# Turning three of the four tiles of x with VectorE instead of TensorE, in a kernel that mixes sliding-window attention with an MLP

## The chip, the cores and the metric

The kernel runs on one core of one Trainium2 chip. The metric is the device time of one execution in microseconds (us). Before the change the median of three executions is 770.48 us (769.53 to 770.53).

## What is computed

The input x has 2048 tokens of 512 features, in float32. Two branches read it and a gate per token mixes them:

```python
g = sigmoid((x * gate_w).sum(-1, keepdims=True))
# branch a: attention, 32 heads of 16 features, causal, a window of 256 tokens
qkv = x @ wqkv                       # (2048, 512) @ (512, 1536)
scores = q @ k.T * 16 ** -0.5        # masked to 0 <= query - key < 256
a = softmax(scores) @ v  @ wo
# branch b: MLP of width 1792
b = gelu(x @ w1 + b1) @ w2 + b2
out = g * a + (1 - g) * b
```

## The kernel before

**Tiles.** The tokens are cut into four tiles of 512 (`T`, numbered t = 0 to 3 in the code, the first to the fourth in the text). Every product that must keep float32 accuracy is taken as three passes: each operand is split into a rounded high part and the remainder as a low part, and `mm3` (lines 89 to 92) issues high x high, high x low and low x high. One call with 512 columns is three matmuls.

**The features must lie on the partitions.** TensorE contracts over partitions, so the projections need x with features on partitions and tokens along the row: `xts[t]`, 4 chunks of 128 features, a high and a low part, 512 tokens. In memory x lies the other way round, token by token. `load_xr` (line 186) loads a tile as four blocks of 128 tokens by 512 features into buffers of the tags `tmp` (three blocks) and `raw` (one block). `qkv_x` (line 191) then, block by block, lets TensorE turn the four 128x128 pieces with an identity (line 204) into one PSUM bank, lets ScalarE copy the bank as the high part (line 208) and VectorE subtract for the low part (line 211). The same four row blocks feed the gate: `gate` (line 216) has `gate_z` (line 228) multiply each with the gate's weights and sum along the row on VectorE, and `gate_end` (line 221) makes g and 1 - g.

**The stage of projections.** `qkv(t)` (line 284) computes for a tile twelve pieces of four `mm3` calls: eight for q and k (line 234), four for v (line 256), numbered n = 0 to 11. Each piece uses one of two PSUM banks of the tag `d`. A q or k piece is taken out by ScalarE (line 248) and VectorE (line 251) into one of eight buffers of the tag `h`, and stored to DRAM (line 252); a v piece by ScalarE (line 271), and stored (line 273). While tile t is projected, the next tile of x is loaded after n = 0 (n = 1 for the first tile), turned after the pieces n in `xat` (5, 7, 8, 9 for the first tile, 4, 6, 8, 10 for the others), and its gate follows. In the first tile the weights come in at the same time: `load_raw` (line 121) loads 256 KB, and `split` (line 140) makes the two parts, high on ScalarE, low on VectorE or GpSimd. The turned tile is also stored to DRAM (`XT`, line 304) for the MLP, which runs later.

**After that.** Attention starts when a set amount of the dense work is done (`START`, `AHEAD`); from there on `fill` interleaves what is left of the dense work, the last tile's projections and the MLP, with attention, and the rest of the output follows. VectorE finds the row maxima of attention (line 399).

**What sets the order.** TensorE, ScalarE, VectorE and GpSimd execute in the order in which the program emits their instructions. Emission is steered by a plan of times: `after(ns, fn)` puts a piece of work so many planned nanoseconds later, `tick` advances the plan. All DMAs are issued by SyncE (SP), in one queue whose order a scheduler chose beforehand; an issue that must wait holds up everything behind it. Each DMA signals one of eight counters in turn, and a DMA waits until the one eight places ahead of it has landed, so at most eight are under way.

Of the kernel before, what the change touches and what calls it, by code (L numbers as in the profile page):

```python
# [9 lines left out]
F32 = mybir.dt.float32  # L10
F32R = mybir.dt.float32r
BF16 = mybir.dt.bfloat16
AF = mybir.ActivationFunctionType
# [4 lines left out]
S, D, F, H, DH, W = 2048, 512, 1792, 32, 16, 256  # L18
T = 512
NT = S // T  # L20
NB = T // 128
NC = D // 128
# [10 lines left out]
def gated_mix(ctx: ExitStack, tc: tile.TileContext, x, wqkv, wo, w1, b1, w2, b2, gate_w, out):  # L33
    nc = tc.nc
    x = x[0]
# [3 lines left out]
    sb = ctx.enter_context(tc.tile_pool(name="sb", bufs=1))  # L39
    dr = ctx.enter_context(tc.tile_pool(name="dr", bufs=1, space=DRAM))  # L40
    ps = ctx.enter_context(tc.tile_pool(name="ps", bufs=1, space=PSUM))
# [3 lines left out]
    def f32(ap):  # L45
        return ap.bitcast(F32)
# [39 lines left out]
    g = cp.tile([128, S // 128], F32, name="g")  # L86
# [8 lines left out]
    now, todo, done = [0.0, 0], [], set()  # L95

    def after(ns, fn, *args):
        now[1] += 1
        heapq.heappush(todo, (now[0] + ns, now[1], fn, args))
# [7 lines left out]
    def tick(ns):  # L107
        now[0] += ns
        while todo and todo[0][0] <= now[0]:
            step_todo()  # L110

    def need(*keys):
        for key in keys:
            while key not in done:
                step_todo()
# [5 lines left out]
    def load_raw(key, early=False):  # L121
        kind, i = key
        src = {"qk": lambda: wk4[:, :, i * 128:(i + 1) * 128],
               "v": lambda: wqkv[i * 128:(i + 1) * 128, 2 * D:3 * D],
               "w1": lambda: w1k[:, :, i * 128:(i + 1) * 128],
               "w2": lambda: w2[i * 128:(i + 1) * 128],
               "wo": lambda: wo[i * 128:(i + 1) * 128]}[kind]()
        if early and kind == "v":
            if i == 0:
                raws["v"] = f32(sb.tile([128, NC, 2, T], F32R, tag="xt", bufs=1, name="raw_v"))  # L130
            raw = raws["v"][:, i, 0]
        elif early:
            raw = sb.tile([128, 2, 320], F32, tag="pt", bufs=PTS, name=f"raw_{kind}{i}")
            raw = raw.rearrange("p a b -> p (a b)")[:, 0:T]
        else:
            raw = sb.tile([128, T], F32, tag="raw", bufs=3, name=f"raw_{kind}{i}")
        nc.sync.dma_start(raw.rearrange("p (c f) -> p c f", c=NC) if len(src.shape) == 3 else raw, src)
        raws[key] = raw

    def split(key, eng):  # L140

        kind, i = key
        raw = raws.pop(key)
        w = sb.tile([128, 2, T], F32R, tag="w", bufs=14, name=f"{kind}_{i}")
        nc.scalar.activation(w[:, 0], raw, AF.Copy)
        wt[key] = w.rearrange("p s (c f) -> p s c f", c=NC) if kind in ("qk", "w1") else w

        def lo():
            eng.tensor_sub(w[:, 1], raw, f32(w[:, 0]))
            done.add(("w", key))  # L150
        after(700, lo)
# [3 lines left out]
    def load(key):  # L155

        paced[0] = max(now[0], paced[0] + PACE)
        after(paced[0] - now[0], load_now, key)
# [17 lines left out]
    def clear_k(i):  # L176

        pr, n = divmod(i, 4)
        for s in range(2):
            v = of_head(ks[:, pr, n * 1024:(n + 1) * 1024], s)  # L180
            nc.scalar.activation(v, nil.unsqueeze(2).unsqueeze(3).broadcast_to([128, 4, 2, 64]), AF.Identity,
                                 bias=own[:, 2 * pr + s:2 * pr + s + 1])

    xts, xrs = {}, {}

    def load_xr(t):
        for b in range(NB):
            xrs[t, b] = sb.tile([128, D], F32, tag=("tmp", "raw")[b // 3], bufs=3, name=f"xr{t}_{b}")
            nc.sync.dma_start(xrs[t, b], x[t * T + b * 128:t * T + (b + 1) * 128])

    def qkv_x(t, b):

        if b == 0:
            if t < NT - 1:
                v = (ks[:, 0], ks[:, 1], qs.rearrange("p a c -> p (a c)"))[t]
                v = v.rearrange("p (c s t) -> p c s t", c=NC, s=2)
            else:
                v = sb.tile([128, NC, 2, T], F32R, tag="xt", bufs=1, name=f"xt{t}")
            xts[t] = v
        xt = xts[t]  # L200
        xr = xrs[t, b]
        p = ps.tile([128, NC, 128], F32, tag="sm", bufs=3, name=f"xp{t}_{b}")
        for c in range(NC):
            nc.tensor.transpose(p[:, c], xr[:, c * 128:(c + 1) * 128], ident)
        tick(4 * 110)

        def hi():
            nc.scalar.activation(xt[:, :, 0, b * 128:(b + 1) * 128], p, AF.Copy)

        def lo():  # L210
            nc.vector.tensor_sub(xt[:, :, 1, b * 128:(b + 1) * 128], p,
                                 f32(xt[:, :, 0, b * 128:(b + 1) * 128]))
            done.add(("x", t, b))
        after(100, hi), after(500, lo)

    def gate(t):
        for b in range(NB):
            after(1500 * b, gate_z, t, b)
        after(6500, gate_end, t)

    def gate_end(t):
        sl = slice(t * NB, (t + 1) * NB)
# [2 lines left out]
        nc.vector.reciprocal(g[:, sl], g1[:, sl])  # L225
        nc.vector.tensor_scalar(g1[:, sl], g[:, sl], -1.0, 1.0, op0=ALU.mult, op1=ALU.add)

    def gate_z(t, b):
        xr = xrs.pop((t, b))
        junk = sb.tile([128, D], BF16, tag="sq", bufs=2, name=f"xj{t}_{b}")  # L230
        nb = t * NB + b
        nc.vector.tensor_tensor_reduce(junk, xr, gwb, 1.0, 0.0, ALU.mult, ALU.add, z[:, nb:nb + 1])
# [44 lines left out]
    def warm(n):  # L277

        p = ps.tile([128, T], F32, tag="d", bufs=2, name=f"warm{now[0]}")
        for _ in range(n):  # L280
            nc.tensor.matmul(p[:, 0:384], idle[:, 0:128], idle, start=True, stop=True)
            tick(160)

    def qkv(t):
        last = t == NT - 1
        qk = [("qk", j) for i in range(NC) for j in (i, i + NC)]
        vs = [("v", b) for b in range(NB)]
        pieces = qk[:2] + vs + qk[2:] if last else qk + vs
        if t == 0:
            keys = qk + [("v", c) for c in range(NC)]  # L290
            load_xr(0)
            for key in keys[0:4]:
                load_raw(key, True)
            warm(WARM[0])
            for b in range(NB):
                qkv_x(0, b)
            warm(WARM[1])
            split(keys[0], nc.vector)
            split(keys[1], nc.vector)
            nc.sync.dma_start(gwb, gate_w.partition_broadcast(128))  # L300
        need(*[("x", t, b) for b in range(NB)])
        for n, (kind, j) in enumerate(pieces):
            if not last and XAT <= n < XAT + NC:
                nc.sync.dma_start(XT[t][n - XAT], f32(xts[t][:, n - XAT]))
            if kind == "qk":
                need(("w", (kind, j)))
            else:
                need(*[("w", ("v", c)) for c in range(NC)])
            if t == 0 and n < 4:
                load_raw(keys[n + 4], True)  # L310
                load_raw(keys[n + 8], True)
            if t == 0 and n == 10:
                nc.sync.dma_start(b1c, b1.rearrange("(f p) -> p f", p=128))
            if kind == "qk":
                yield from qkv_qk(t, j)
            else:
                yield from qkv_v(t, j)
            if t == 1 and n % 3 == 2:
                clear_k(n // 3)
            if t == 2 and n in (1, 3, 5, 7):  # L320
                clear_k(4 + n // 2)
            if t == 2 and n in (2, 4):
                load_k(0, n // 2 - 1, slice(0, 1))
            if t == 2 and n in (9, 10):
                load_k(0, n - 9, slice(1, 2))
            if t == 0:
                for i in ([2], [3], [4], [5], [6], [7, 8], [9, 10], [11])[n] if n < 8 else []:
                    split(keys[i], nc.vector if i % 2 else nc.gpsimd)
                if n == 1:
                    gate(0)  # L330
                    load_xr(1)
            elif n == 0 and not last:
                load_xr(t + 1)
            if last and n not in (4, 5):
                load(later.pop(0))
            if last and n == len(pieces) - 1:
                for _ in range(4):
                    load(later.pop(0))
            xat = (5, 7, 8, 9) if t == 0 else (4, 6, 8, 10)
            if not last and n in xat:  # L340
                qkv_x(t + 1, xat.index(n))
            if not last and n == xat[-1] + 1:
                gate(t + 1)


    vts, Ms, pts, pvs = {}, {}, {}, {}
# [484 lines left out]
```

## Time and profile before

| | |
|---|---|
| median of three executions | 770.48 us |
| span of the profiled execution (first to last instruction) | 769.0 us |
| TensorE busy | 749.8 us, 98% of the span |
| VectorE busy | 533.7 us, 69% |
| ScalarE busy | 432.9 us, 56% |
| GpSimd busy | 384.1 us, 50% |
| DMA, first 40 us | 94% and 98% of the 16 engines' time in the two halves |
| granted TensorE clock, mean | 0.998 |

The profile gives the span of its own execution, 769.0 us; the time around the span is not on its page. The median of the runs is 1.48 us above that span. In the rows of the profile PE is TensorE's matmuls, PEld its weight loads, DVE VectorE, ACT ScalarE, POOL GpSimd and SPq the queue of SyncE, which issues the DMAs. A matmul's duration is modelled and overlaps the next one: successive matmuls of 512 columns start 0.227 us apart, though each is shown with some 0.39 us.

### The profile page before, as it was taken

Reading aid. Unit: us, or ns where it says so; the run is one execution under the profiler, and the core shown is the slowest. Engines: PE = TensorE matmul, PEld = TensorE weight load, DVE = VectorE, ACT = ScalarE, POOL = GpSimd, SP = SyncE. Lnnn points to the kernel's source line nnn. Section 1 sums busy time; section 2 is a strip of 40 time slices with the busy share of each in tenths; the row PEclk is TensorE's granted clock in tenths of the full one; section 3 lists DMA queues with packets and bytes.
Section 4 is the critical chain, followed back from the end, with each engine's and each line's share of the span. In section 5 each row is a group of like instructions: output and inputs, shape, how many; then the busy total and the mean of one; then the engine's idle time right before and its main releaser. Section 6 shows DMA issues by size and latency. Waiting matters only on the chain.

```text
span 769.0 us, 18430 instructions
## 1 busy us (share of the span) xinstructions
PE 749.8 (98%) x6102; PEld 625.0 (81%) x6102; DVE 533.7 (69%) x1548; ACT 432.9 (56%) x945; POOL 384.1 (50%) x1125
## 2 busy tenths in 40 slices
PE   8999999989999999999999999999999999999998
PEld 6888888867888888788878877888888788878877
DVE  4532332889669868976897799679868886893543
ACT  4434433358458646754875577447646754775641
POOL 2200000018656765766567667657765675777300
PEclk9999999999999999999999999999999999999999
DMA  9986856755643565565346756643476474537483
GB/s 290 362 300 202 312 184 215 259 189 171 179 119 72 183 185 148 145 208 148 97 111 162 204 160 199 183 126 94 162 202 164 115 213 123 128 107 211 165 261 110
DMA packets 136559, 137.81 MB, mean 179 GB/s; under 512 B 53264, under 2 KB 88592, under 8 KB 136464
## 3 DMA queue, kind: packets, MB, share of 16 engines
q1 hardware_dynamic: 136464, 136.64, 59.8%
q8 instruction: 48, 0.79, 0.4%
q14 instruction: 47, 0.39, 0.2%
HBM read 82.58 MB, written 54.00 MB: 178 GB/s over the span
## 4 chain that ended last, share of the span: by engine, by line
PE 86%; DVE 8%; issue 3%; ACT 2%; DMA 1%; SPq 0%; DVEq 0%; ACTq 0%
PE sm L394 10%; PE st L435 8%; PE y L90 7%; PE y L91 6%; PE y L92 6%; PE u L90 6%; PE u L91 5%; PE u L92 5%; PE pv_st L476 5%; PE pv_sm L476 4%; PE qk L92 4%; PE qk L90 4%; PE qk L91 4%; DVE jm L399 4%; PE a L90 2%
## 5 line engine op out<-in xcount | busy, mean ns | idle before, releaser
L399 DVE CUSTOM_DVE_ANT_0 jm<-sm,mask 128x384 bf16<-128x384 f32 (+2 forms) x512 | 269.9, 527 | 67.4 <-PE sm L394 38.7
L450 ACT ACTIVATE pt<-st 128x320 f32<-128x320 f32 (+4 forms) x512 | 206.0, 421 | 133.9 <-PE st L435 127.8
L441 POOL TENSOR_SCALAR_AFFINE_SELECT pt<-pt 64x128 f32<-64x128 f32 x512 | 176.5, 345 | 188.7 <-ACT pt L450 168.6
L394 PE MATMUL sm<-ks,qs 96*128 96x384 f32 (+2 forms) x512 | 172.2, 339 | 10.4 <-DVE M L399 8.5
L435 PE MATMUL st<-qs,ks 128*128 128x320 f32 (+4 forms) x512 | 155.5, 305 | 0.7 <-ACT pt L450 0.7
L444 POOL TENSOR_SCALAR_AFFINE_SELECT pt<-pt 64x128 f32<-64x128 f32 x448 | 154.3, 344 | 0.0
L394 PEld LDWEIGHTS sm<-ks,qs 96*128 96x128 f32 x512 | 96.6, 189 | 43.7 <-DVE M L399 20.6
L435 PEld LDWEIGHTS st<-qs,ks 128*128 128x128 f32 x512 | 97.7, 191 | 18.2 <-ACT pt L450 1.1
L90 PE MATMUL y<-w,h 128*128 128x512 f32 x224 | 90.2, 403 | 0.0
L91 PE MATMUL y<-w,h 128*128 128x512 f32 x224 | 88.4, 395 | 0.0
L92 PE MATMUL y<-w,h 128*128 128x512 f32 x224 | 87.7, 391 | 0.0
L419 POOL CAST qs<-tt 8x256 fp32r<-8x256 f32 x128 | 61.0, 477 | 46.5 <-PE u L92 38.1
L90 PE MATMUL u<-mx,w 128*128 128x512 f32 x196 | 80.4, 410 | 0.0
L91 PE MATMUL u<-mx,w 128*128 128x512 f32 x196 | 77.3, 394 | 0.0
L92 PE MATMUL u<-mx,w 128*128 128x512 f32 x196 | 76.8, 392 | 0.0
L476 PE MATMUL pv_st<-pt,vbuf 64*32 64x320 f32 (+4 forms) x1408 | 73.5, 347 | 0.0
L476 PE MATMUL pv_sm<-pt,vbuf 64*32 64x320 f32 (+4 forms) x1408 | 73.0, 347 | 0.0
L476 PEld LDWEIGHTS pv_st<-pt,vbuf 64*32 64x32 f32 x1408 | 56.4, 106 | 4.7
L476 PEld LDWEIGHTS pv_sm<-pt,vbuf 64*32 64x32 f32 x1408 | 53.9, 106 | 7.5 <-issue 2.1
L251 DVE TENSOR_TENSOR qke<-qk,qke 128x512 fp32r<-128x512 f32 x32 | 22.1, 690 | 48.9 <-ACT qke L248 40.5
L248 ACT ACTIVATE qke<-qk 128x512 fp32r<-128x512 f32 x32 | 19.1, 598 | 55.9 <-PE qk L92 37.0
L92 PEld LDWEIGHTS y<-w,h 128*128 128x128 f32 x224 | 42.1, 188 | 9.7
(124 smaller groups left out, 1314.2 us busy)
## 6 DMA issues: line engine op xcount, KB each, us to landing
mx<-XT SPq DMA_DIRECT2D x24, 512.0 KB
SQ<-qke SPq DMA_DIRECT2D x16, 512.0 KB
SK<-qke SPq DMA_DIRECT2D x16, 512.0 KB
qs<-SQ SPq DMA_DIRECT2D x32, 256.0 KB
ND<-nd SPq DMA_DIRECT2D x32, 256.0 KB
ks<-SK SPq DMA_DIRECT2D x112, 64.0 KB
raw_w<-in_B_w_dram SPq DMA_DIRECT2D x28, 256.0 KB
SV<-vx SPq DMA_DIRECT2D x16, 272.0 KB
```

The costliest lines, as they stand in the source:

```text
L90: nc.tensor.matmul(p, lh, rh, start=first, stop=False)
L91: nc.tensor.matmul(p, lh, rl, start=False, stop=False)
L92: nc.tensor.matmul(p, ll, rh, start=False, stop=last)
L251: nc.vector.tensor_sub(e[:, 1 - h], p, f32(e[:, h]))
L394: nc.tensor.matmul(p[:, :w], qs[0:96, pr, b * 128:(b + 1) * 128], of_head(ks[0:96, pr, 2 * k0:2 * (k0 + w)], s), start=True, stop=True)
L399: nc.vector.tensor_tensor_reduce(junk[:, :w], p[:, :w], mask[:, 384 - w:384], 1.0, -3e38, ALU.add, ALU.max, M[:, b % RB, i:i + 1])
L419: nc.gpsimd.tensor_copy(dst, tt[32 * i:32 * i + 8].unsqueeze(1).broadcast_to([8, 2, RB, 32]))
L435: nc.tensor.matmul(p[:, :w], ks[:, pr, 2 * k0:2 * k0 + 128], qs[:, pr, k0:k0 + w], start=True, stop=True)
L441: nc.gpsimd.affine_select(out=v[:, :, 0:64], in_=v[:, :, 0:64], pattern=[[0, 2], [1, 64]], compare_op=ALU.is_ge, fill=0.0, base=0, channel ...
L444: nc.gpsimd.affine_select(out=v[:, :, W:W + 64], in_=v[:, :, W:W + 64], pattern=[[0, 2], [-1, 64]], compare_op=ALU.is_ge, fill=0.0, base=- ...
L450: nc.scalar.activation(pt[:, pr, :w], p[:, :w], AF.Exp, scale=SCALE)
L476: nc.tensor.matmul(pv[r // 64][32 * i:32 * i + 32, q - c * T:e - c * T], vs(i, r), rhs(r), start=start, stop=last, skip_group_check=True, ...
```

## The change

The first tile of x is loaded and turned as before. For the other three, `load_xq(t)` loads x in another shape: for each chunk of 128 features one buffer of 128 partitions by 512 numbers, filled by four DMAs of 32 partitions. Such a DMA takes 32 features of all 512 tokens as 16 squares of 32 tokens by 32 features and lays them side by side; a square's row is 32 numbers, 128 bytes, in one piece. VectorE's transposition turns each 32x32 square in place of its own (`turn`), which leaves features on partitions and tokens along the row, in a buffer of the tag `x1`. From there ScalarE makes the high and VectorE the low part, per chunk of features rather than per block of tokens.

The row blocks are no longer there for the gate, so `gate_row(t, b)` loads each again, as 128 tokens by 512 features into a buffer of the tag `ya`, after the pieces n = 1, 3, 5, 7 of tile t's own projections (one tile later than before), and plans its `gate_z` 4000 ns later. The gate's weights occupy one of the two `ya` buffers until the last `gate_z`.

```diff
-    def load_xr(t):
+    def load_xr():
         for b in range(NB):
...
+    def load_xq(t):
+
+        for c in range(NC):
+            xrs[t, c] = xq = sb.tile([128, T], F32, tag=("tmp", "raw")[c // 3], bufs=3, name=f"xq{t}_{c}")
+            src = x[t * T:(t + 1) * T, c * 128:(c + 1) * 128]
+            for a in range(4):
+                nc.sync.dma_start(xq[32 * a:32 * a + 32].rearrange("r (n k) -> r n k", k=32),
+                                  src[:, 32 * a:32 * a + 32].rearrange("(n r) k -> r n k", r=32))
...
+    def qkv_x(t, c):
+
+        xt, xq = x_tile(t), xrs.pop((t, c))
+        xs = sb.tile([128, T], F32, tag="x1", bufs=2, name=f"xs{t}_{c}")
+
+        def turn():
+            nc.vector.transpose(xs, xq)
+
+        def hi():
+            nc.scalar.activation(xt[:, c, 0], xs, AF.Copy)
+
+        def lo():
+            nc.vector.tensor_sub(xt[:, c, 1], xs, f32(xt[:, c, 0]))
+            done.add(("x", t, c))
+        after(100, turn), after(900, hi), after(1600, lo)
+
+    def gate_row(t, b):
+
+        xrs[t, b, "g"] = sb.tile([128, D], F32, tag="ya", bufs=2, name=f"xg{t}_{b}")
+        nc.sync.dma_start(xrs[t, b, "g"], x[t * T + b * 128:t * T + (b + 1) * 128])
+        after(4000, gate_z, t, b, xrs.pop((t, b, "g")))
+        if b == NB - 1:
+            after(5500, gate_end, t)
...
                 if n == 1:
-                    gate(0)
-                    load_xr(1)
+                    gate0()
+                    load_xq(1)
             elif n == 0 and not last:
-                load_xr(t + 1)
+                load_xq(t + 1)
...
             if not last and n in xat:
                 qkv_x(t + 1, xat.index(n))
-            if not last and n == xat[-1] + 1:
-                gate(t + 1)
+            if t > 0 and n in (1, 3, 5, 7):
+                gate_row(t, n // 2)
```

The first tile's turning, called `qkv_x0` in the changed kernel, and its gate, `gate0`, do what `qkv_x` and `gate` did.

More of the change, by code (lines that the diff above doesn't have):

```diff
@@ L184, in gated_mix, with x_tile @@
     xts, xrs = {}, {}
-    def load_xr(t):
+    def load_xr():
         for b in range(NB):
[L188 to L193, printed above, removed]
+            xrs[0, b] = sb.tile([128, D], F32, tag=("tmp", "raw")[b // 3], bufs=3, name=f"xr0_{b}")
+            nc.sync.dma_start(xrs[0, b], x[b * 128:(b + 1) * 128])
+    def load_xq(t):
[5 more added lines that the diff above has]
+                                  src[:, 32 * a:32 * a + 32].rearrange("(n r) k -> r n k", r=32))
+    def x_tile(t):
+        if t not in xts:
             if t < NT - 1:
@@ L199, in qkv_x, with qkv_x0 @@
             xts[t] = v
-        xt = xts[t]
-        xr = xrs[t, b]
-        p = ps.tile([128, NC, 128], F32, tag="sm", bufs=3, name=f"xp{t}_{b}")
+        return xts[t]
+    def qkv_x0(b):
+        xt, xr = x_tile(0), xrs[0, b]
+        p = ps.tile([128, NC, 128], F32, tag="sm", bufs=3, name=f"xp{b}")
         for c in range(NC):
@@ L212, in lo, with gate0 @@
                                  f32(xt[:, :, 0, b * 128:(b + 1) * 128]))
-            done.add(("x", t, b))
+            done.add(("x", 0, b))
         after(100, hi), after(500, lo)
-    def gate(t):
+    def qkv_x(t, c):
[15 more added lines that the diff above has]
+            after(5500, gate_end, t)
+    def gate0():
         for b in range(NB):
-            after(1500 * b, gate_z, t, b)
-        after(6500, gate_end, t)
+            after(1500 * b, gate_z, 0, b, xrs.pop((0, b)))
+        after(6500, gate_end, 0)
     def gate_end(t):
@@ L226, in gate_end, with gate_z @@
         nc.vector.tensor_scalar(g1[:, sl], g[:, sl], -1.0, 1.0, op0=ALU.mult, op1=ALU.add)
-    def gate_z(t, b):
-        xr = xrs.pop((t, b))
+    def gate_z(t, b, xr):
         junk = sb.tile([128, D], BF16, tag="sq", bufs=2, name=f"xj{t}_{b}")
@@ L290, in qkv @@
             keys = qk + [("v", c) for c in range(NC)]
-            load_xr(0)
+            load_xr()
             for key in keys[0:4]:
@@ L295, in qkv @@
             for b in range(NB):
-                qkv_x(0, b)
+                qkv_x0(b)
             warm(WARM[1])
```

## The prediction, made before the changed kernel ran

> **What bounds the kernel now.** I read the page's shares first, then the slices over the span, then the chain that ended last in the stretch that the change touches.
>
> ```profile
> span 769.0 us, 18430 instructions
> PE 749.8 (98%) x6102; PEld 625.0 (81%) x6102; DVE 533.7 (69%) x1548; ACT 432.9 (56%) x945; POOL 384.1 (50%) x1125
> PE   8999999989999999999999999999999999999998
> PEclk9999999999999999999999999999999999999999
> DMA  9986856755643565565346756643476474537483
> ```
>
> TensorE is busy nearly throughout at full granted clock, so time taken out of its stream is worth its full length unless something else becomes late. But the DMA engines are nearly full in the first slices (a slice is 19.2 us). The same by stage, as busy us of each engine, granted clock, DMA share and GB/s:
>
> ```profile
> 0.00:20.00 20.00, 17.47 (x71) 12.60 (x72) 9.31 (x16) 8.70 (x14) 5.24 (x18) 1.00 0.94 295
> 20.00:40.00 20.00, 20.00 (x98) 16.53 (x97) 9.95 (x18) 9.38 (x20) 4.61 (x7) 1.00 0.98 349
> 40.00:60.00 20.00, 20.00 (x92) 16.55 (x91) 7.25 (x18) 6.73 (x16) 0.47 (x3) 1.00 0.83 300
> 60.00:80.00 20.00, 20.00 (x95) 16.55 (x94) 6.25 (x13) 9.00 (x20) 0.16 (x1) 1.00 0.63 203
> 132.00:162.00 30.00, 30.00 (x140) 25.27 (x140) 24.21 (x78) 11.29 (x20) 1.58 (x4) 1.00 0.68 218
> ```
>
> TensorE has no gap from 20 to 80 us; VectorE and ScalarE are under half busy; the DMA share is 0.98, then 0.83. So TensorE bounds the projections, with the DMA engines right behind it in the first tile. At the start of attention (last row) VectorE is at 24.2 of 30 us.
>
> The chain that ended last shows what the three later tiles' transpositions cost (start, us, what):
>
> ```profile
> 26.45 0.44 PE xp L204 x4
> ...
> 110.64 0.44 PE xp L204 x4
> ```
>
> There are twelve such rows between 26 and 111 us, four for each of three tiles, each on the chain.
>
> **The change, part by part.**
>
> **Twelve groups of transpositions go: -5.3 us.** The matmuls around one group, as start and duration:
>
> ```profile
> 26.06 0.39 PE L92 MATMUL qk<-ks,qk 128*128 128x512 f32 x1
> 26.29 0.60 PE L204 MATMUL xp<-ident,xr 128*128 128x128 f32 x4
> 26.64 0.48 PE L90 MATMUL qk<-ks,qk 128*128 128x512 f32 x1
> 26.96 0.39 PE L91 MATMUL qk<-ks,qk 128*128 128x512 f32 x1
> 29.48 0.39 PE L90 MATMUL qk<-ks,qk 128*128 128x512 f32 x1
> 44.54 0.39 PE L90 MATMUL qk<-ks,qk 128*128 128x512 f32 x1
> ```
>
> A matmul starts 0.23 us after another. Without the group the L91 row would stand at 26.52, not 26.96: 0.44 us, as the chain says, times 12. The row at 29.48 is the first matmul of piece n = 7 (weight qk7), which comes to 29.04 without the group before it; that at 44.54 starts the second tile's projections, 42.78 without its four groups.
>
> **What a square load costs the DMA engines.** Before, such a tile is four loads of 256 KB. Now it is 16 loads of 64 KB, each 512 pieces of 128 bytes, besides four gate rows of 256 KB. The trace has no such load. The nearest are the loads of v for attention, in pieces of 136 bytes, which run alone in these two windows; the third is a full stretch of large stores:
>
> ```profile
> 74.00:75.00 1.00, 1.00 (x7) 0.81 (x6) 0.00 (x0) 0.09 (x1) 0.00 (x0) 1.00 0.64 87
> 227.50:228.50 1.00, 1.00 (x7) 0.87 (x6) 0.86 (x4) 0.38 (x1) 0.53 (x2) 1.00 0.30 54
> 26.00:28.00 2.00, 2.00 (x12) 1.66 (x12) 0.88 (x2) 1.51 (x4) 0.76 (x1) 1.00 1.04 402
> ```
>
> First window: 0.64 x 16 engines x 1 us = 10.2 us for 87 KB, 640 pieces: 16.0 ns each. Second: 4.8 us for 397 pieces: 12.1 ns. Upper end: weights in pieces of 512 bytes, from SP's issues, each of which waits for the DMA eight places ahead:
>
> ```profile
> 6.99 0.43 SPq L137 DMA_DIRECT2D raw_qk<-in_A_wqkv_dram  x1
> 7.47 0.69 SPq L137 DMA_DIRECT2D raw_v<-in_A_wqkv_dram  x1
> 12.36 0.38 SPq L137 DMA_DIRECT2D raw_qk<-in_A_wqkv_dram  x1
> 13.26 0.53 SPq L137 DMA_DIRECT2D raw_v<-in_A_wqkv_dram  x1
> 14.05 1.84 SPq L304 DMA_DIRECT2D XT<-ks  x3
> 16.32 0.68 SPq L252 DMA_DIRECT2D SQ<-qke  x1
> ```
>
> The issues at 12.36, 13.26 and 14.05 mark the landings of the 9th, 10th and 11th DMA, 0.85 us apart per 256 KB: 26.6 ns for 512 bytes. Between 12.1, 16.0 and 26.6 I take the mean, 18.2 ns, nearest to the 16.0 row but above it, since a square's pieces lie 64 KB apart where v's lie 2 KB apart. One square load d = 512/16 x 18.2 ns = 0.58 us (0.39 to 0.85). Three tiles: 28 us of all 16 engines instead of about 8.
>
> The Trainium skill gives a rule for this (DMA: Bandwidth & Descriptors, section "Why small descriptors are slow"): about 3 fixed cycles per packet on top of one per 32 bytes. Scaled from the 26.6 ns row that is 7/19, an estimate of 9.8 ns; d would be 0.31 and the sum below -4.7 us. The trace speaks against part of it: for 136 bytes it gives 11.2 where the windows show 12.1 and 16.0.
>
> **First tile: weight qk7 comes late, +4.9 us.** In the changed order the 14th DMA and the three behind it are square loads; then come weight qk3 and a v block, a store of q, the other twelve square loads, a store of k, a store of x, and only then weight qk7 and the last v block; before, these were the 17th and 18th. The row at 16.32 marks the 14th landed at about 16.3, so the 13th at about 15.4. From there, one queue without a pause: 16 d, two blocks at 0.85, three stores of 524 KB at 402 GB/s = 1.3 each, qk7 itself 0.85: it lands at 21.85 + 16 d = 31.2. After that:
>
> ```profile
> 24.26 0.62 ACT L145 ACTIVATE qk<-raw_qk 128x512 fp32r<-128x512 f32 x1
> 24.78 0.62 ACT L145 ACTIVATE v<-raw_v 128x512 fp32r<-128x512 f32 x1
> 26.49 0.60 ACT L248 ACTIVATE qke<-qk 128x512 fp32r<-128x512 f32 x1 [1.08 <-PE qk L92]
> 27.12 0.69 DVE L251 TENSOR_TENSOR qke<-qk,qke 128x512 fp32r<-128x512 f32 x1 [1.97 <-ACT qke L248]
> 27.72 0.68 DVE L149 TENSOR_TENSOR qk<-raw_qk,qk 128x512 fp32r<-128x512 f32 x1
> ```
>
> The order stays: high part of qk7 at 24.26, a v weight, piece 5's copy, its low part, then qk7's low part. All that queues behind the landing: 0.52 + 0.52 + 0.60 + 0.1 + 0.61 + 0.68 = 3.0 us, against which the first matmul, on the high part, gains 0.25. Piece 7 starts at 31.2 + 2.75 = 33.95 instead of 29.04: 4.9 us (1.7 at the low price, 9.2 at the high).
>
> **Second and third tile: gate rows behind squares, +0.85 us each.** SP issues 14 of a tile's 16 square loads behind the store of the last v block, then a q store, then the first gate row; VectorE stands at `gate_z` until it lands, with the low part of piece 3 behind it, whose bank piece 5 needs.
>
> ```profile
> 45.51 0.33 SPq L273 DMA_DIRECT2D SV<-vx  x1
> 0.80 1.81 SPq L189 DMA_DIRECT2D xr<-in_A_x_dram  x4
> 3.98 1.94 PE L204 MATMUL xp<-ident,xr 128*128 128x128 f32 x8 [0.28 <-DMA xr<-in_A_x_dram]
> L232 DVE CUSTOM_DVE_ANT_0 xj<-xr,gwb x16: 677/682/689, 13.8 to 117.8; 128x512 bf16<-128x512 f32 x16
> L382 SPq DMA_DIRECT2D vbuf<-SV x64: 573/607/1025, 72.4 to 708.4; - x64
> ```
>
> From the tile's start T the last v store is issued at 45.51 - 44.54 = 0.97; then 14 d, 1.3 for the store, 0.65 for the row, about 2.1 until data count as landed (an estimate: 3.98 - 0.80 less 0.4 of issue and 0.65 of data), 0.68 for `gate_z` and 0.61 for the low part: T + 6.3 + 14 d = 14.45 at d = 0.58. Piece 5 wants to start at 5 x 12 x 0.227 = 13.6: 0.85 us, in two tiles 1.7 (0 at 16.0 ns and below, 4.6 each at the high price). An issue takes SP up to 0.61 us (last row), so SP alone would set nearly the same pace. The later gate rows wait for each other's `gate_z` (one free buffer) and queue behind three stores each; about 0.5 us of room is left.
>
> **Hidden, taken at nothing.** Twelve turns on VectorE: a turn of 128 columns is in the trace,
>
> ```profile
> L414 DVE STREAM_TRANSPOSE tt<-nm x32: 311/311/314, 149.8 to 693.2; 128x128 f32<-128x128 f32 x32
> ```
>
> and one of 512, at a column per cycle as VectorE's other instructions here, is about 0.71 us (0.31 if length were free, 1.24 if it were four turns): 8.5 us under TensorE's 93, where VectorE has 10 of 20 us free. The high part reads the turned copy: 0.62 against 0.60 us, also hidden. The x stores and the loads of k move back in SP's queue; attention reads k from about 132 us, tens of us later; were that room gone, each us late would be a us. The fourth tile's gate moves to where attention begins: three VectorE instructions of 0.61 plus 0.5 at the end, of which about 2 us fall into 132 to 162, where the row above leaves 5.8 free: 0, at most 2.0.
>
> **Sum:** -5.3 + 4.9 + 1.7 = +1.3 us on the profiled span of 769.0. The median, 770.48, is 1.48 above that span; I carry this over: 771.8 us.
>
> **The rivals.**
>
> *The gain arrives.* If a piece costs 12.1 ns, qk7 is only 1.7 us late and no gate row waits: -3.6, 766.9 us. For it: the second window, and that v's pieces are so alike. Against: the first window; at 16.0 ns it is -5.3 + 3.7 = -1.6, 768.9, about the point from which it decides. The skill's packet rule would end here, at 765.8.
>
> *The squares choke the queue.* If 128 bytes take as long as 512, 26.6 ns, qk7 costs 9.2 and the gate rows 4.6 each: +13.1, 783.6 us. For it: reads of 128 bytes at a pitch of 64 KB, which no row shows. Against: 136 bytes never cost that here. The Trainium skill speaks for it (same page, "Specifications"): transfers reach line rate from 512 bytes on. No run here shows 128-byte squares yet.
>
> *VectorE becomes the bound where attention begins.* If the fourth tile's gate instructions or the waits for its rows take 2 us of 132 to 162 without using idle time, 2.0 comes on top: 773.8 us. For it: 81% busy there. Against: 5.8 us idle.
>
> That the transpositions stay is excluded: TensorE's order in the changed program holds only the first tile's.
>
> **How the numbers follow.** A time within 0.2% (1.5 us) of before cannot be told from no change. The forecast, with squares between about 15 and 21 ns, has 0.40, from 768.5 to 775, of which 0.03 lies on the faster side, 0.16 within the bound and 0.21 above. The gain arriving has 0.32, 0.30 of it faster. The choked queue has 0.20 and VectorE 0.08, both slower. Faster 0.33, same 0.18, slower 0.49. The range goes from 766.0, just under the low price, to 781.0, which leaves out most of the high price's worst; about 1.5 in 10 stay outside.
>
> **What would show it.** Right: twelve groups fewer on the chain; TensorE idle for some us at about 29 us before line 90, released by qk7's split; VectorE idle before `gate_z` for a gate row in tiles 2 and 3; a DMA share near 1 from 2 to 55 us at a rate far below 400 GB/s while squares load. Wrong: no TensorE gap before 120 us (squares are cheap), or gaps at other places, above all at the turns, if a square load lands after its turn's place.

## The result, and the profile after

The changed kernel takes 780.14 us, median of four executions (777.99 to 784.86), against 770.50 (769.53 to 774.44) for the kernel before on the same chip: a ratio of 1.0104, with a 95% interval of 1.0072 to 1.0136. It is slower by about 8 us (1.04% of 770.5). The prediction had 771.8 with a range of 766.0 to 781.0. The sign that had most of the chance came, and the time is just inside the range, but it lies far above the forecast and outside the forecast's own 768.5 to 775. One execution in the experiments, of the removal alone, took 1080.7 us at a granted clock of 0.62 and is left out of that kernel's figures.

The profiled execution of the changed kernel is the longest of its four, 784.86 us; its span is 783.1, 14.1 more than the span before. Where these 14.1 us arise is read off the first matmul of attention (`sm`). In the groups of instructions that write this tile, in the kernel before and then after, the figures behind the count are the durations in ns (least, median, most) and the first and the last start in us within the first 200 us:

```profile
L394 PE MATMUL sm<-ks,qs x61: 223/338/690, 132.7 to 199.6; 96*128 96x384 f32 x53, 96*128 96x128 f32 x4, 96*128 96x256 f32 x4
```

```profile
L428 PE MATMUL sm<-ks,qs x51: 223/338/451, 143.2 to 197.9; 96*128 96x384 f32 x43, 96*128 96x128 f32 x4, 96*128 96x256 f32 x4
```

Attention starts 10.5 us later, at 143.2 instead of 132.7. So the loss lies in the projections, ahead of attention. The other 3.6 us are near the end. In the waits of TensorE (us in total, times, longest), the last stage's wait for VectorE, before and after:

```profile
PE a L90 <- DVE ao L720: 1.1, 1, 1.1
```

```profile
PE qk L90 <- DVE qke L285: 9.8, 4, 4.2
...
PE a L90 <- DVE ao L754: 3.0, 1, 3.0
```

The wait at `a` goes up to 5.7 us in the profiled executions of this study, whose programs do not differ near the end; I do not put it down to the change, and compare the start of attention instead. That is one execution of each kernel, and it carries some variation of its own: the first matmul of the projections, ahead of all that differs, starts between 8.16 and 9.71 us in these traces (9.20 before, 8.17 in the changed kernel). The wait of `qk` for `qke` is new, 9.8 us in four pieces.

The page's shares and slices of the changed kernel, as shown of before:

```profile
span 783.1 us, 18395 instructions
PE 750.9 (96%) x6054; PEld 623.0 (80%) x6054; DVE 540.8 (69%) x1560; ACT 434.2 (55%) x945; POOL 384.4 (49%) x1125
PE   8798979998999999999999999999999999999988
DMA  9969696965664556466345766643475374536572
```

TensorE has 48 instructions fewer, the twelve groups of four. Its slices show holes in the second, fourth and sixth, where none was. The DMA slices go up and down. By stage (busy us of each engine, granted clock, DMA share, GB/s):

```profile
20.00:40.00 20.00, 15.82 (x62) 12.28 (x61) 10.33 (x17) 7.12 (x14) 4.84 (x7) 0.91 0.94 317
...
60.00:80.00 20.00, 17.68 (x71) 14.09 (x71) 9.89 (x22) 7.61 (x15) 0.61 (x4) 0.91 0.98 362
...
100.00:120.00 20.00, 17.16 (x66) 13.43 (x67) 8.84 (x21) 7.66 (x15) 0.78 (x5) 0.91 0.93 334
```

In these three stretches TensorE's busy time is short by 2.3 to 4.2 of 20 us, and the clock is 0.91 where it was 1.00. The gaps themselves, from TensorE's instructions in order of time (start, duration, what; in brackets the idle time ahead and what ended it):

```profile
32.43 0.50 PE L90 MATMUL qk<-ks,qk 128*128 128x512 f32 x1 [4.18 <-DVE qke L285]
...
34.22 0.63 PE L92 MATMUL qk<-ks,qk 128*128 128x512 f32 x1
34.65 0.63 PE L90 MATMUL qk<-ks,qk 128*128 128x512 f32 x1
...
64.14 0.70 PE L90 MATMUL qk<-ks,qk 128*128 128x512 f32 x1 [2.33 <-DVE qke L285]
...
100.21 0.50 PE L90 MATMUL qk<-qs,qk 128*128 128x512 f32 x1 [1.51 <-DVE qke L285]
...
107.78 0.50 PE L90 MATMUL qk<-qs,qk 128*128 128x512 f32 x1 [1.82 <-DVE qke L285]
...
115.91 0.50 PE L90 MATMUL v<-v,qs 128*128 128x512 f32 x1 [0.80 <-ACT vx L305]
```

The gap at 32.43 is ahead of piece 7 of the first tile (weight qk7); that at 64.14 is in the second tile; the last three are in the third. Together they are 10.64 us. Behind three of them (4.18, 2.33 and 1.82) matmuls of 512 columns start 0.43 us apart, as at 34.22 and 34.65, instead of 0.227, until TensorE has worked some 3.5 to 4.5 us again. Counted over all starts behind the gaps, less 0.227 each, that is 1.95 + 1.71 + 1.72 us and 0.1 each behind the other two: 5.6 us. The account of the 10.5: -5.3 for the twelve groups, -0.8 because piece 7 could have started at 32.43 - 4.18 = 28.25 instead of 29.04 (the projections of this execution began 1.03 us earlier, as said), +10.64 of gaps, +5.6 of half clock, in all +10.1. The remaining 0.4 I leave open.

The gaps' causes are in the queues of VectorE and ScalarE. VectorE's instructions that stood longest for a gate row in the second and third tile:

```profile
62.78 0.69 DVE L266 CUSTOM_DVE_ANT_0 xj<-xg,gwb 128x512 bf16<-128x512 f32 x1 [5.00 <-DMA xg<-in_A_x_dram]
...
63.39 0.69 DVE L285 TENSOR_TENSOR qke<-qk,qke 128x512 fp32r<-128x512 f32 x1
...
98.85 0.69 DVE L266 CUSTOM_DVE_ANT_0 xj<-xg,gwb 128x512 bf16<-128x512 f32 x1 [4.18 <-DMA xg<-in_A_x_dram]
...
105.82 0.69 DVE L266 CUSTOM_DVE_ANT_0 xj<-xg,gwb 128x512 bf16<-128x512 f32 x1 [4.47 <-DMA xg<-in_A_x_dram]
...
113.64 0.69 DVE L266 CUSTOM_DVE_ANT_0 xj<-xg,gwb 128x512 bf16<-128x512 f32 x1 [4.72 <-DMA xg<-in_A_x_dram]
```

At 63.39 the low part of a piece (`qke`) begins as soon as `gate_z` is done, and at 64.14 TensorE goes on: the product of the gate, which nobody needs yet, holds up what TensorE needs. In the first tile it is the weight: ScalarE stands for it until 30.02, with the copy of piece 5 behind it, whose bank piece 7 needs, so that the last to release piece 7 is piece 5's low part (`qke`). ScalarE's row at the landing, and then SP's queue:

```profile
30.02 0.63 ACT L145 ACTIVATE qk<-raw_qk 128x512 fp32r<-128x512 f32 x1 [6.57 <-DMA raw_qk<-in_A_wqkv_dram]
```

```profile
15.63 7.20 SPq L197 DMA_DIRECT2D xq<-in_A_x_dram  x12
...
24.92 0.82 SPq L137 DMA_DIRECT2D raw_qk<-in_A_wqkv_dram  x1
...
49.48 8.35 SPq L197 DMA_DIRECT2D xq<-in_A_x_dram  x14
...
58.41 0.43 SPq L246 DMA_DIRECT2D xg<-in_A_x_dram  x1
...
96.64 2.34 SPq L395 DMA_DIRECT2D ks<-SK  x3
...
101.42 0.72 SPq L246 DMA_DIRECT2D xg<-in_A_x_dram  x1
```

SP issues a square load every 0.60 us (7.20/12 and 8.35/14). Weight qk7 is issued only at 24.92, the second tile's first gate row at 58.41. The last two rows are loads of k and the third tile's second gate row.

### The profile page after: what moved, and what is told of

The parts are those of the page before. It is cut to its first block, busy times and chain, and to the rows that moved or that the text cites. A ratio compares the mean times of both kernels' runs of the same rounds, so it can differ in the third digit from the quotient of the medians.

```text
span 783.1 us, 18395 instructions
## 1 busy us (share of the span) xinstructions
PE 750.9 (96%) x6054; PEld 623.0 (80%) x6054; DVE 540.8 (69%) x1560; ACT 434.2 (55%) x945; POOL 384.4 (49%) x1125
## 4 chain that ended last, share of the span: by engine, by line
PE 72%; DMA 9%; DVE 8%; SPq 4%; issue 4%; ACT 2%; DVEq 0%; POOL 0%; ACTq 0%; POOLq 0%
PE sm L428 10%; PE st L469 7%; PE y L90 6%; PE y L91 5%; PE y L92 5%; PE u L90 5%; PE u L91 5%; PE u L92 5%; PE pv_st L510 4%; DVE jm L433 4%; PE pv_sm L510 4%; PE qk L90 3%; PE qk L92 2%; PE qk L91 2%; DMA RD<-den 2%
```

## The experiments

The theory (A): TensorE bounds the projections, the removal is worth its length, and the loss comes from waits behind late weights and late gate rows. The rivals are in the expectations. Starts of attention are from each profiled execution; ratios are to the kernel before on the same chip.

### The weights ahead of the squares

The first of the two waits alone is removed.

```diff
                 if n == 1:
                     gate0()
+                if n == 3:
                     load_xq(1)
...
-            xat = (5, 7, 8, 9) if t == 0 else (4, 6, 8, 10)
+            xat = (7, 8, 9, 10) if t == 0 else (4, 6, 8, 10)
```

> The second tile's square loads are issued after the last weights (after piece 3 instead of piece 1) and turned two pieces later (after pieces 7 to 10). Theory A (late weight qk7, and TensorE's half clock behind the gap): the gap of 4.2 us at 28 us goes, and with it about 2.0 us of slow matmuls: some 6 us less than the changed kernel, 774 us. The gaps behind gate rows at 62, 99 and 106 us stay. Rival B (the small pieces fill the DMA queue whatever the order): qk7 is in time, but the second tile's x or the stores are late instead, a gap of 3 us or more appears between 35 and 50 us, and the time stays near 780.

Measured: 778.55 us (774.23 to 780.08), before 772.92 (770.36 to 776.06); ratio 1.0064 [1.0044, 1.0084]. TensorE is busy from 20 to 40 us without a gap, and attention starts at 136.0, 7.2 earlier than in the changed kernel. But this profiled execution, 774.23, is the fastest of the ten; by the ratios the gain on the changed kernel is 0.40%, 3 us, and theory A's 774 did not come as the median. The gate rows' wait stays:

```profile
PE qk L90 <- DVE qke L285: 6.3, 3, 3.6
```

The first gap is the late weight. The other gaps do not come from it.

### The gate rows later

```diff
-            if t > 0 and n in (1, 3, 5, 7):
-                gate_row(t, n // 2)
+            if t > 0 and n in (5, 7, 9, 11):
+                gate_row(t, n // 2 - 2)
```

> The gate's rows are loaded after pieces 5, 7, 9 and 11 instead of 1, 3, 5 and 7, when the next tile's square loads are over; nothing else changes. Theory A: VectorE no longer stands at the gate for a row behind square loads; the gaps at 62, 99 and 106 us (2.3, 1.5, 1.8 and 0.8 us) and the slow matmuls behind them (about 4 us) go: some 10 us less than the changed kernel, 770 us, with the gap at 28 us still there. Rival B (the DMA queue is full at that time in any order): the rows are late at the new places too, and the time stays above 776.

Measured: 779.49 us (774.57 to 783.62); ratio 1.008 [1.0049, 1.0111]. The waits of TensorE between 20 and 145 us:

```profile
PE qk L90 <- DVE qke L285: 5.1, 1, 5.1
PE qk L91 <- DVE xt L239: 1.8, 1, 1.8
PE v L90 <- ACT vx L305: 1.6, 2, 0.8
PE v L90 <- DVE qke L285: 0.9, 1, 0.9
```

The first gap, 5.1 us, is left, since the weights load as in the changed kernel. Those that the rows had made are gone, but there are new ones of 4.3 us together, at the v pieces and at the turned x of the fourth tile (`xt`, line 239). The rows still come late, now in front of other work in VectorE's queue. Moving the wait does not remove it: theory A's 770 did not come, and rival B is right for these places.

### Both orders

> Both orders together: square loads of the second tile after the weights, gate rows after the square loads. Theory A: no gap on TensorE between 10 and 130 us, no half clock, and the 5.3 us of transpositions are gained: 764 to 766 us, faster than the kernel before. Rival B: the extra DMA traffic keeps at least one gap of 2 us, 770 us or more.

Measured: 773.66 us (770.60 to 776.72); ratio 1.0008 [0.9986, 1.0031], no difference from before. Attention starts at 133.9. Theory A's 764 to 766 did not come: the gaps of the late weight are gone, but waits at the v pieces and at the turned x stay.

```profile
PE v L90 <- DVE qke L285: 2.1, 2, 1.4
PE v L90 <- ACT vx L305: 1.6, 2, 0.8
PE qk L91 <- DVE xt L239: 1.5, 1, 1.5
```

Gate rows stand ahead of two of these. In the third tile VectorE stands 7.18 us for one, with low parts behind it, which TensorE gets 1.37 us late at 106.41; the 1.51 at the turned x follow a stand of 3.68 us for another:

```profile
104.45 0.69 DVE L266 CUSTOM_DVE_ANT_0 xj<-xg,gwb 128x512 bf16<-128x512 f32 x1 [7.18 <-DMA xg<-in_A_x_dram]
...
114.56 0.69 DVE L266 CUSTOM_DVE_ANT_0 xj<-xg,gwb 128x512 bf16<-128x512 f32 x1 [3.68 <-DMA xg<-in_A_x_dram]
```

### Row loads in the squares' places

```diff
-            src = x[t * T:(t + 1) * T, c * 128:(c + 1) * 128]
-            for a in range(4):
-                nc.sync.dma_start(xq[32 * a:32 * a + 32].rearrange("r (n k) -> r n k", k=32),
-                                  src[:, 32 * a:32 * a + 32].rearrange("(n r) k -> r n k", r=32))
+            nc.sync.dma_start(xq, x[t * T + c * 128:t * T + (c + 1) * 128])
```

> As the changed kernel, but each 128 KB x 2 buffer of the later tiles is filled by one load of 128 rows of 2 KB instead of four loads of squares; the turned x of tiles 2 to 4 is then not x's transpose, and the output is not the reference's. VectorE's turns, the gate's separate rows and all else stay. Theory A (the cost of the square loads makes the weight and the gate rows late): both kinds of gap go or fall under 1 us, 765 to 768 us. Rival C (VectorE's turns or the separate gate rows themselves hold up the banks): gaps at 62, 99 and 106 us stay, 774 us or more.

Measured: 765.44 us (764.32 to 768.29); ratio 0.9915 [0.9883, 0.9947]. TensorE has no gap in the projections, and attention starts 5.5 us earlier than before, at 127.2:

```profile
L425 PE MATMUL sm<-ks,qs x67: 223/338/525, 127.2 to 199.4; 96*128 96x384 f32 x56, 96*128 96x128 f32 x7, 96*128 96x256 f32 x4
```

This settles the main point. VectorE's twelve turns and the twelve separate gate rows are still in this kernel and make no gap; the whole loss is the way the squares load, and what they push back.

### The removal alone

```diff
+        if t == 0:
             p = ps.tile([128, NC, 128], F32, tag="sm", bufs=3, name=f"xp{t}_{b}")
             for c in range(NC):
                 nc.tensor.transpose(p[:, c], xr[:, c * 128:(c + 1) * 128], ident)
             tick(4 * 110)
+        else:
+            p = xr.rearrange("p (c k) -> p c k", c=NC)
```

> The kernel before, with TensorE's transpositions of the second to fourth tile left out: the high and low parts are taken from the row blocks as they are, so what is computed from these tiles is not the reference's. All DMAs and the gate stay as before. This prices the removal alone. Theory A (TensorE is the bound, each of the twelve groups is worth its 0.44 us on the chain): 5.3 us less than the kernel before, 765 to 766 where before is at 770.5, and the start of attention earlier by the same 5.3 us. Rival B (part of these 0.44 us is covered by something that ends as late, for instance the weights or the parts of x): 2 to 4 us less, with new TensorE gaps in the first 120 us.

Measured: 770.12 us (nine executions, 767.94 to 773.85), before 774.54 (770.37 to 777.09); ratio 0.9946 [0.9923, 0.997], 4.2 us less. The same kernel once more, for its trace:

> Once more the kernel before without the twelve groups of transpositions (the tiles two to four taken as they are, so not the reference's numbers), for its trace at full granted clock. If the groups are worth their 0.44 us each on the chain, no TensorE gap before 130 us and the start of attention at about 132.7 - 5.3 = 127.4 us; if something else holds TensorE there, gaps in the first 130 us and a start between 128.5 and 132.

It took 770.29 us, one execution, beside a median of 771.6 for before. Attention starts at 129.5, 3.2 earlier than before and not 5.3; TensorE has two gaps in the first tile:

```profile
30.06 0.50 PE L92 MATMUL qk<-ks,qk 128*128 128x512 f32 x1 [0.82 <-DVE qk L149]
35.76 0.50 PE L91 MATMUL v<-v,ks 128*128 128x512 f32 x1 [0.87 <-DVE v L149]
```

Here rival B is right in part: without its four groups in the first tile TensorE runs into the low parts of two weights, and 1.7 of the 5.3 us go there.

### The clock kept up

```diff
+    def idle_mm(k):
+
+        p = ps.tile([128, T], F32, tag="sm", bufs=3, name=f"idle{now[0]}")
+        for _ in range(k):
+            nc.tensor.matmul(p[:, 0:384], idle[:, 0:128], idle, start=True, stop=True)
+
+    FILL = {(0, 7): 24, (1, 5): 12}
...
+            if (t, n) in FILL:
+                idle_mm(FILL[t, n])
```

> The changed kernel, with idle matmuls of 384 columns put into TensorE's stream ahead of piece 7 of the first tile (24 of them, about 3.9 us at 0.16 us each) and ahead of piece 5 of the second tile (12, about 1.9 us), where TensorE stood idle; their result is read by nobody. Theory D (a gap of about 2 us or more makes the granted clock fall to half for 3 to 4 us, and these us are lost besides the gap): the matmuls that follow piece 7 of the first tile and piece 5 of the second start 0.23 us apart instead of 0.43, the granted clock in the slices of 30 to 40 and 60 to 70 us is near 1.00, attention starts about 3.5 us earlier than in the changed kernel and the time is about 3.5 us less, 776 to 777 where the changed kernel is at 780. Rival E (the matmuls behind a gap are slow for another reason, their operands or the DMA traffic): the spacing stays at 0.43 and the time stays within 1 us of the changed kernel or goes above it.

Measured: 782.54 us (779.54 to 784.35), before 774.54; ratio 1.0100 [1.0065, 1.0134], the changed kernel's own ratio within the intervals. The stretch behind the first gap, in the changed kernel and in this one:

```profile
28.00:36.00 8.00, 3.82 (x12) 2.58 (x11) 4.24 (x6) 4.19 (x8) 3.06 (x6) 0.85 1.01 390
```

```profile
28.00:36.00 8.00, 8.00 (x42) 5.10 (x41) 4.09 (x6) 4.32 (x9) 3.08 (x6) 1.00 1.02 398
```

The clock is 1.00, and behind both places matmuls soon start 0.23 us apart: theory D is right about the mechanism. About its price it is not. TensorE gets to piece 5 of the second tile sooner and then waits for the same gate row:

```profile
63.94 0.50 PE L90 MATMUL qk<-ks,qk 128*128 128x512 f32 x1 [1.63 <-DVE qke L285]
```

Piece 5 starts at 63.94 instead of 64.14, although 1.95 us of half clock ahead of it are gone. Attention starts at 141.2, 2.0 us earlier, where 3.5 were expected (2.6 if both are counted from their first matmul of the projections, 8.74 and 8.17); 2 us are less than the intervals tell apart, and the time shows no gain. While the DMA queue sets when a gate row lands, half clock ahead of it is time that would be waited anyway. In this run no stretch of half clock is left in the projections; the third went too, as the gaps of the third tile are 1.45 us and less. So the 5.4 us of the three stretches, which my account adds up in full, are worth 2.0 to 2.6.

### Gate rows in pairs, with room

```diff
     def gate_row(t, b):
 
-        xrs[t, b, "g"] = sb.tile([128, D], F32, tag="ya", bufs=2, name=f"xg{t}_{b}")
-        nc.sync.dma_start(xrs[t, b, "g"], x[t * T + b * 128:t * T + (b + 1) * 128])
-        after(4000, gate_z, t, b, xrs.pop((t, b, "g")))
-        if b == NB - 1:
-            after(5500, gate_end, t)
+        xg = f32(sb.tile([128, 2, T], F32R, tag="h", bufs=8, name=f"xg{t}_{b}"))
+        for i in range(2):
+            nc.sync.dma_start(xg[:, i], x[t * T + (b + i) * 128:t * T + (b + i + 1) * 128])
+            after(9000 + 1400 * i, gate_z, t, b + i, xg[:, i])
+        if b == NB - 2:
+            after(12000, gate_end, t)
...
-            if t > 0 and n in (1, 3, 5, 7):
-                gate_row(t, n // 2)
+            if t > 0 and n in (1, 4):
+                gate_row(t, n // 4 * 2)
```

With this and the weights ahead of the squares:

> The changed kernel with the squares of the second tile loaded after n = 3 instead of n = 1 (as in the run with the weights first), and with the gate rows taken in two pairs, into buffers of the tag h, after the pieces n = 1 and n = 4, each row with its product planned 9000 ns after its load instead of 4000. Theory A (all that is lost beside the removed transpositions is waits behind late weights and late gate rows): no TensorE gap over 0.5 us in the first 130 us, 765 to 767 where before is at 770.5. Rival F (the queue of SP is too full in the third and fourth quarter of the projections, so that whatever is moved, something else there comes late: the turned x or a v block): gaps of 1 to 5 us in all between 90 and 130 us at other lines, 768 to 774.

Measured: 769.14 us (765.27 to 772.07), before 774.54; ratio 0.9933 [0.9905, 0.9962]. This is the full computation, and it beats both kernels. One gap above 0.4 us is left between 20 and 130 us, and attention starts at 128.2:

```profile
62.77 0.50 PE L90 MATMUL qk<-ks,qk 128*128 128x512 f32 x1 [0.46 <-DVE qke L286]
```

```profile
L430 PE MATMUL sm<-ks,qs x66: 223/338/447, 128.2 to 199.7; 96*128 96x384 f32 x56, 96*128 96x128 f32 x6, 96*128 96x256 f32 x4
```

Rival F falls: the queue has room, once nothing that is needed late stands ahead of what is needed early. The rows moved alone, with the squares after n = 1 as in the changed kernel:

> The changed kernel with the gate rows alone moved, in pairs into buffers of the tag h and with their products 9000 ns after the load, as in the run with the rows apart; the squares of the second tile stay after n = 1. Theory A (late weight and late gate rows are separate causes whose losses add): the gap before piece 7 of the first tile is there, 4 to 5 us, with half clock behind it for some 3.5 us (1.7 to 2 us lost), and no other gap over 0.5 us before 130 us; attention starts 6 to 7 us later than with both moved, at 134 to 135.5 us, 2 to 3 us later than in the kernel before; the time is 0.2 to 0.4% above before. Rival B (one delay swallows the other, as late rows cost nothing once everything is late): attention starts as in the changed kernel less at most 3 us, at 140 or later, 0.8% or more above before.

Measured: 774.05 us (770.36 to 778.74), before 771.60 (769.91 to 775.43); ratio 1.0027 [0.9996, 1.0059], not told from before. Its one wait in the projections, and its start of attention, a little ahead of theory A's 134 to 135.5 and far from rival B's 140:

```profile
PE qk L90 <- DVE qke L286: 4.1, 1, 4.1
```

```profile
L429 PE MATMUL sm<-ks,qs x60: 223/338/447, 133.4 to 199.3; 96*128 96x384 f32 x52, 96*128 96x128 f32 x4, 96*128 96x256 f32 x4
```

The four starts of attention make a table of both causes:

| start of attention, us | gate rows with room | gate rows as changed |
|---|---|---|
| weights ahead of squares | 128.2 | 136.0 (+7.8) |
| squares ahead of weights | 133.4 (+5.2) | 143.2 (+15.0) |

Alone the weights cost 5.2 us and the gate rows 7.8, together 15.0. Each start is that of one execution, and the one of 136.0 is the fastest of its ten, the one of 143.2 the longest of its four. By the ratios of the times to before, the weights alone cost 0.94% (7.2 us), the gate rows alone 1.31% (10.1) and both 1.71% (13.2), each known to some 0.4%. So both are causes of their own. Whether the two losses add is not settled: the starts give 2.0 us more than the sum, the times 4.1 less, with an uncertainty as large.

### Smaller squares

```diff
             for a in range(4):
-                nc.sync.dma_start(xq[32 * a:32 * a + 32].rearrange("r (n k) -> r n k", k=32),
-                                  src[:, 32 * a:32 * a + 32].rearrange("(n r) k -> r n k", r=32))
+                to = xq[32 * a:32 * a + 32].rearrange("r (n k) -> r n k", k=32)
+                fr = src[:, 32 * a:32 * a + 32].rearrange("(n r) k -> r n k", r=32)
+                for i in (0, 8):
+                    nc.sync.dma_start(to[:, i:i + 8], fr[:, i:i + 8])
```

> The changed kernel with each square load cut into two, of 8 squares instead of 16: 32 DMAs of 32 KB and 256 pieces per tile instead of 16 of 64 KB and 512 pieces. The pieces and their places stay the same. Theory G (the pace of the squares is set per piece, by the engines or by the writing of the descriptors): an issue takes SP about 0.30 us instead of 0.60 where it waits for nothing, the squares of a tile take as long as in the changed kernel, and the time is within 2 us of it. Rival H (the pace is set per DMA, by the issue or by the eight under way): an issue stays at 0.5 to 0.6 us, the squares take up to twice as long, 8 us more per tile, and the gaps before piece 7 and at the gate rows grow by several us each: 790 us or more.

Measured: 805.16 us (798.62 to 808.74), before 774.54; ratio 1.0393 [1.0334, 1.0452]. SP's queue:

```profile
17.02 12.92 SPq L200 DMA_DIRECT2D xq<-in_A_x_dram  x24
...
51.12 0.33 SPq L200 DMA_DIRECT2D xq<-in_A_x_dram  x1
...
56.18 15.69 SPq L200 DMA_DIRECT2D xq<-in_A_x_dram  x29
```

In a train, a load with half the pieces takes 0.54 us (12.92/24, 15.69/29) where one with all took 0.60: the pace is set per DMA, rival H. The engines are not what limits it; with nothing but squares under way their share is 0.40:

```profile
60.00:70.00 10.00, 8.49 (x38) 6.70 (x36) 1.38 (x2) 3.62 (x6) 0.00 (x0) 1.00 0.40 62
```

An issue by itself takes 0.33 us (the row at 51.12; 0.42 for a whole square load, at 44.04 in the changed kernel), so writing the descriptors is not the whole 0.54 either. Eight issues at 0.54 are 4.3 us; if a square load takes about that long to land, the wait for the DMA eight places ahead sets the pace. That fits, but is only argued: no run varied how many may be under way, and issuing squares from a second queue was not tried.

## Why the prediction was right in sign and wrong in size

**The twelve groups, -5.3: right.** Row loads in the squares' places gave 5.5. That the groups lay on the chain did not mean that nothing was close behind: with the removal alone, low parts of weights took 1.7 back.

**A square load, 0.58 us: right value, wrong reason.** It is 0.60. But I had it from 18.2 ns per piece on the engines. Where only squares load in the changed kernel:

```profile
52.00:57.00 5.00, 5.00 (x24) 4.14 (x23) 1.03 (x2) 2.36 (x4) 0.00 (x0) 1.00 0.80 128
87.00:94.00 7.00, 7.00 (x32) 5.81 (x31) 1.40 (x3) 3.06 (x6) 0.00 (x0) 1.00 0.70 125
```

0.80 x 16 x 5 us = 64 us for 640 KB, 5000 pieces: 12.8 ns each; the second window gives 11.5. That is the low end of my three rows, 12.1, by which the rival of the arriving gain had 766.9. Yet that rival did not come true, since the engines' share is not what paces a train of small DMAs; nor did the sign of a share near 1 while squares load, which is 0.80 and 0.70. That 18.2 ns of engine time gave the pace of the queue is luck. The Trainium skill's packet rule (DMA: Bandwidth & Descriptors, "Why small descriptors are slow"), scaled to an estimate of 9.8 ns, is nearer to the measured 11.5 to 12.8 than my 18.2, but the 765.8 that went with it did not come.

**Weight qk7, +4.9: right step, slightly too large.** Forecast to land at 31.2 and piece 7 to start at 33.95, 4.9 us late; it had landed by 30.02, piece 7 started at 32.43, and the gap is 4.18. The order behind the landing was as forecast, 2.41 us against 2.75, though what ended the wait last was piece 5's low part, not qk7's split. The step lacked what half clock adds: with the rows out of the way the weights cost 5.2 by the start of attention.

**Gate rows, +0.85 each: the step that failed.** They made gaps of 2.33 us in the second tile and 1.51 + 1.82 + 0.80 = 4.13 in the third, 6.5 instead of 1.7, and 7.8 with all that follows. (The 0.80 is ended by ScalarE's copy of a v piece; it is counted here because it is absent where the rows have room, but its cause is not traced.) Two parts were wrong. The term for the row's landing was too small: the second tile's start is 64.14 - 2.33 - 13.6 = 48.2; the first row was issued 10.2 us behind it, as forecast, but took 4.4 us from its issue at 58.41 to its product, where the forecast allowed 0.65 + 2.1 = 2.75. All eight rows of the second and third tile took 3.6 to 5.4 us. And "about 0.5 us of room is left" for the later rows did not hold in the third tile. The first row's product frees the buffer at 99.47, but SP, which had begun to issue six loads of k at 96.64, comes to the second row only at 101.42, behind the last two of these and two stores; it lands 4.4 us later, and the gap of 1.82 follows. Four more loads of k, 3.15 us from 104.08, stand ahead of the third row, issued at 108.27. I had asked of the loads of k only whether they themselves come too late.

**Turns on VectorE, 0.71 us, hidden: right.** Their group in the changed kernel:

```profile
L233 DVE STREAM_TRANSPOSE xs<-xq x12: 698/702/712, 24.1 to 119.8; 128x512 f32<-128x512 f32 x12
```

**The fourth tile's gate, 0: right.** In the 30 us from the new start of attention, VectorE is busy 26.6 us instead of 24.2, and TensorE has no gap:

```profile
142.00:172.00 30.00, 30.00 (x141) 25.29 (x140) 26.61 (x87) 10.99 (x20) 1.58 (x4) 1.00 0.83 254
```

**Missing: the clock.** I added gaps as if TensorE went on at full clock. Three of the five are followed by half clock, 5.4 us in the trace; the run with idle matmuls, without it, starts attention 2.0 to 2.6 us earlier.

**The rivals.** The choked queue has the nearest time, 783.6, but not its mechanism: a piece never cost 26.6 ns. The queue is choked by the number of DMAs. VectorE as the bound did not appear. That the time lies inside the range is luck: the upper end reached 781.0 for the sake of pieces at 26.6 ns, while the sum had +1.3 us where the start of attention alone moved by 10.5.

## What to carry to other kernels

Price a train of small DMAs per DMA, not per byte or piece alone: 0.60 us with 512 pieces, 0.54 with 256. Then go down each in-order queue behind it and ask of every entry not only when it is needed, but what stands behind it: an operand that nobody needs yet, waited for in VectorE's queue, cost 7.8 us here by the start of attention (10.1 by the times), and planning its use 9 instead of 4 us behind its load, in pairs with buffers of their own, took that away. Behind gaps of 2.33 us and more TensorE ran at half clock for some us; where another wait came next, most of that time would have been waited anyway (5.4 us in the trace were worth 2.0 to 2.6).

## What had not been expected of the hardware

The granted clock of TensorE falls after quite short gaps. Over the projections of all kernels here, gaps of up to 1.63 us were never followed by half clock; of three gaps between 1.76 and 1.82 us two were (the one began it only after three matmuls at full spacing, the other after six); those of 2.33 us and more all were. The matmuls behind then start 0.43 instead of 0.227 us apart, and full clock is back 3.5 to 6 us behind the gap's end. The Trainium skill (TensorE: Matmul & The Clock Gate, "Part 1: The HAM clock gate (the "warmup" mystery)") tells of half clock after an idle window of about 3.4 us, by a window that runs freely, and asks (same page, "Why this matters for your kernels") for no gaps over about 3 us. The time until full clock is back and the varying onset agree with it; the gaps of 1.76 and 1.82 us that set it off do not.
